# Forward stores moved to the sync queue and partly merged; phi's derivative rebuilt on GpSimd in the backward

## The chip, the cores and the metric

The kernel runs on one core of a Trainium2 chip. The core has a matrix engine (TensorE, PE), a vector engine (VectorE, DVE), a scalar engine for activations (ScalarE, ACT), a general engine (GpSimd, POOL) and a sync engine (SyncE, SP) that only issues DMAs. Every engine works through its own list of instructions in order; semaphores tie the lists together. DMAs are issued from SP and from ACT, each with a queue of its own, and are carried by 16 shared DMA engines. The metric is the device time of one execution in microseconds. A change of less than about 0.5% (12 us) can't be told from no change here.

## What is computed

Four attention blocks in a row on a sequence of 2048 tokens with 640 features (32 heads of 20), and then the gradients of all of it: of the input and of four weight matrices. Blocks 0 and 2 are linear attention (A), blocks 1 and 3 causal attention with a window of 256 (B). All data are bf16.

```python
def _A_ref(x, wqkv, wo):
    ...
    q, k, v = qkv[0], qkv[1], qkv[2]
    phi = lambda t: jnp.where(t > 0, t + 1, jnp.exp(t)) + 1e-6
    pq, pk = phi(q), phi(k)
    kv = jnp.einsum("bhsd,bhse->bhde", pk, v)
    z = jnp.einsum("bhsd->bhd", pk)
    num = jnp.einsum("bhqd,bhde->bhqe", pq, kv)
    den = jnp.einsum("bhqd,bhd->bhq", pq, z)[..., None] + 1e-6
    o = num / den
    return (lambda x, *d: x.transpose(*d))(o, 0, 2, 1, 3).reshape(B, S, D) @ wo
...
x = x + _A_ref(_layernorm(x, axis=-1), A_wqkv, A_wo)
x = x + _B_ref(_layernorm(x, axis=-1), B_wqkv, B_wo)
x = x + _A_ref(_layernorm(x, axis=-1), A_wqkv, A_wo)
x = x + _B_ref(_layernorm(x, axis=-1), B_wqkv, B_wo)
...
_out, _vjp = jax.vjp(_f, A_x, A_wqkv, A_wo, B_wqkv, B_wo)
_grads = _vjp(grad_out)
```

The derivative of phi is 1 where its argument is positive and exp of it elsewhere, that is min(exp(t), 1).

## The kernel before

The tokens are cut into 16 tiles of 128. Everything that the backward needs is written to DRAM by the forward and read back tile by tile.

**Forward** (`forward`), one program of about 806 us. `a_first` runs layer 0's layer norm and q, k, v over all tiles: the exponential of the projection goes to a tile `ee` (ACT, L457), is capped at 1 there (DVE, L458; the result is phi's derivative), and phi is put together from the two (L461) into `pp` for q and into the resident `pk` for k; v goes to the resident `vv`. `a_kv` sums the key-value products of all tiles into `mbd`. Then `ab_pass(0)` goes over the tiles once more and interleaves, for tiles some steps apart: layer 0's numerators (`a_num`), the output projection, layer 1's layer norm, q, k, v (`b_qkv`), its scores and values (`attn`: scores on PE into the PSUM ring `s_ps`, exponential on ACT at L617, masks on POOL and DVE, values on PE), its output projection, and `a_first` for layer 2. After a second `a_kv`, `ab_pass(2)` does the same without a following linear layer and stores the output x.

Nine kinds of store per tile are issued from ACT: pq, eq, pk, ek and v of a linear layer, its output o and the reciprocals `r32` of its denominators, and for a windowed layer o and the reciprocals `linv`. SP issues the stores of the layer norms `hn` and of `qkvp`, and all transposing DMAs (*flips*) that bring a tile into the layout that PE takes as weights: `hnTA`, `pqT`, `oTA`, `hnTB`, `QT`, `KT`, `oTB`, and `wT` for the transposed weights.

**Backward.** A short phase for layer 3's output projection (806 to 870 us), `B_attn_bwd(3)`, the phase `bwd_phase(3, 2, 1)`, `B_attn_bwd(1)`, and `bwd_phase(1, 0, None)`. Within such a phase, `lin_grads` of the linear layer reads tmp_dN, pk and v through flips (`dNT`, `pkT`, `vT`) and eq and ek by plain loads, multiplies the products by eq and ek on DVE (L1181) into `dqkv`; `tail` flips `dqkv` (`dqT`), multiplies it by the transposed weight `wq` (30 matmuls per tile, L839) into `dh`, and runs the layer norm's gradient: DVE L995, ACT L1002, POOL L1005 (`gw`), DVE L1007 (`gcar`). In layer 2's phase `local_dO` of layer 1 follows in the same loop, with POOL L1055 (`prod`); in layer 0's, the result is stored.

**What sets the order.** Each of the phases is written as a list of operations with reads and writes. A planner (`Sched.order`) gives every operation an assumed duration, simulates the five engines and one DMA channel, and emits the operations in the order in which they would start; each engine then keeps this order. For a DMA issue it assumes a time on the issuing engine: 1100 ns plus size for a flip, 330 ns for a copy on SP and 200 ns for one on ACT. An instruction that waits for its data holds up all that stands behind it on its engine.

Of the kernel before, what the change touches and what calls it, by code (L numbers as in the profile page):

```python
# [11 lines left out]
ALU = mybir.AluOpType  # L12
# [4 lines left out]
P = 128  # L17
# [15 lines left out]
def dve_ns(n):  # L33
    return 150 + 1.04 * n
# [26 lines left out]
class Sched:  # L61
# [39 lines left out]
    def order(self):  # L101
# [21 lines left out]
        while len(out) < len(self.ops):  # L123
# [50 lines left out]
class Kern:  # L174
    def __init__(self, ctx, tc, x0, A_wqkv, A_wo, B_wqkv, B_wo, grad_out, outs):
# [61 lines left out]
        self.ckv = self.const.tile([P, 3, 4 * DH], F32, name="ckv")  # L237
        nc.vector.memset(self.ckv[:, 0:2, :], self.c_att)
        nc.vector.memset(self.ckv[:, 2, :], 1.0)
# [69 lines left out]
    def forward(self):  # L309
# [4 lines left out]
        hch = CW // DH  # L314
        with ExitStack() as st:
# [5 lines left out]
            def ring(name, n, shape, dt=BF, **kw):  # L321
# [17 lines left out]
                wT=ring("wT", 1, [P, DT, P]), rt=ring("rt", 2, [P, H], F32), li=ring("li", 2, [P, H], F32),  # L339
            )  # L340
            pk = big.tile([P, TT, D], BF, name="pk")
            vv = big.tile([P, TT, D], BF, name="vv")
# [11 lines left out]
                   (("Wqkv_B", QT), ("Wqkv_A", QT), ("Wo_A", D), ("Wo_B", D))}  # L354
            S = Sched(tc, ahead=AHEAD)
# [79 lines left out]
            def a_qkv(l, tt, hnT):  # L435
# [3 lines left out]
                def chunk(ci):  # L439
                    def f():  # L440
# [4 lines left out]
                        if ci >= 4:  # L445
# [66 lines left out]
            def a_num(l, tt, oT):  # L512
                sv = self.sv[l]
                o = R["oA"].buf()
                rt = R["rt"].buf()

                def chunk(ci):
                    def f():
# [16 lines left out]
                        if ci == 0:  # L535
                            op("DVE", 190, lambda: nc.vector.tensor_scalar_add(rt.t, ps.t[:, CW:CW + H], 1e-6), [ps],
                               [rt])
                            op("DVE", 190, lambda: nc.vector.reciprocal(rt.t, rt.t), [], [rt])
                            dma("ACT", lambda: self.tm_view(sv["r32"])[:, tt, :], lambda: rt.t, 16 * KB, [rt], [])
# [3 lines left out]
                            in1=rt.t[:, ci * hch:(ci + 1) * hch].unsqueeze(2).to_broadcast([P, hch, DH]), op=ALU.mult),  # L543
                           [ps, rt], [(o, ci)])
# [53 lines left out]
            def attn(l, b, qT, kTs, vts, oT):  # L598
# [3 lines left out]
                pvs, lv, es = {}, R["li"].buf(), {}  # L602
# [918 lines left out]
```

## Time and profile before

| | us |
|---|---|
| median of 3 runs (lowest to highest) | 2367.98 (2361.93 to 2374.64) |
| span of the profiled execution | 2364.9 |
| PE, DVE, ACT, POOL busy | 2054.9, 1472.1, 1219.0, 850.2 |
| forward up to the last x store | about 806 |
| layer 3's projection phase | about 806 to 870 |
| attention backward, layers 3 and 1 | about 870 to 1190 and 1610 to 1960 |
| linear stage of layer 2 with layer 1's projection | about 1410 to 1540 |
| linear stage of layer 0 | about 2185 to 2305 |

A timeline row of the profile gives the start and the duration in microseconds, the engine, the line of the kernel, the operation, the tiles written and read, their shapes and how many instructions are merged; in brackets stands how long the engine had been idle and what ended that. ACTq and SPq are DMA issues of these engines; they are not counted as busy time. A DMA row of the list of issues gives the size of one and the median time from issue to landing. PE is busy 87% of the span, but each stage has its own limit, so the stages are read one by one.

### The profile page before, as it was taken

The numbers are of one execution on the slowest core, as the hardware profiler recorded it, in microseconds if no ns is written. First come the engines' busy times: TensorE is split into PE (matmuls) and PEld (weight loads), VectorE is DVE, ScalarE is ACT, GpSimd is POOL, SyncE is SP. The second block draws the span as 40 slices with busy tenths as digits, with TensorE's granted clock in tenths as the row PEclk, the third lists the DMA queues.
The fourth block names the chain that finished last, engine by engine and source line by source line (L and its number), as shares of the span: only waits on it lengthen the run. The fifth ranks groups of instructions, "written<-read, shape, count | busy, mean of one in ns | idle before, by whom it ended". The sixth has DMA issues, their size and how long they took to land. (4 is left out here: it accounts for less than half of the span.)

```text
span 2364.9 us, 68753 instructions
## 1 busy us (share of the span) xinstructions
PE 2054.9 (87%) x28146; PEld 1428.7 (60%) x28146; DVE 1472.1 (62%) x3120; ACT 1219.0 (52%) x1837; POOL 850.2 (36%) x1851
## 2 busy tenths in 40 slices
PE   5778888878888789898889979997989888997899
PEld 3555555555555457777756657754777775664664
DVE  5656676655565479989943328812998994443552
ACT  3527777716777328888822213312888882210330
POOL 1014454504555445555512203301555551220120
PEclk9989999989999789999999999997999998998999
DMA  7659999726666766777687779736666677878963
GB/s 245 196 134 194 202 212 204 178 93 151 138 151 139 188 178 131 125 130 130 136 173 177 163 189 208 166 94 151 130 126 134 124 139 154 192 178 193 189 153 102
DMA packets 937070, 377.91 MB, mean 160 GB/s; under 512 B 817072, under 2 KB 921136, under 8 KB 936496
## 3 DMA queue, kind: packets, MB, share of 16 engines
q1 hardware_dynamic: 856672, 299.45, 60.9%
q10 hardware_dynamic: 80080, 74.06, 9.7%
q8 instruction: 220, 3.60, 0.7%
q14 instruction: 98, 0.80, 0.1%
HBM read 115.34 MB, written 114.95 MB: 97 GB/s over the span
## 5 line engine op out<-in xcount | busy, mean ns | idle before, releaser
L1342 ACT ACTIVATE e_sb<-pair 128x768 bf16<-128x768 f32 x480 | 389.0, 812 | 123.7 <-PE pair L1322 116.0
L1357 DVE TENSOR_TENSOR ds_sb<-pair,e_sb 128x768 bf16<-128x768 f32 x480 | 436.4, 948 | 17.9 <-PE pair L1322 13.5
L617 ACT ACTIVATE e_sb<-s_ps 128x1536 bf16<-128x1536 f32 (+2 forms) x256 | 350.8, 1370 | 86.2 <-PE s_ps L612 42.9
L621 POOL TENSOR_SCALAR_AFFINE_SELECT e_sb<-e_sb 128x256 bf16<-128x256 bf16 x512 | 217.9, 448 | 491.1 <-ACT e_sb L617 467.0
L839 PE MATMUL mm_ps<-wq,dqT 128*128 128x320 bf16 x1920 | 284.9, 304 | 20.7 <-DMA dqT<-dqkv 20.7
L839 PEld LDWEIGHTS <-om 128*128 128x128 bf16 x1920 | 190.3, 100 | 166.5 <-DMA om<-o 9.9
L1349 POOL TENSOR_SCALAR_AFFINE_SELECT e_sb<-e_sb 128x256 bf16<-128x256 bf16 x448 | 182.1, 406 | 272.2 <-ACT e_sb L1342 263.6
L839 PE MATMUL mm_ps<-dqkv,om 128*128 128x480 bf16 x1280 | 270.8, 369 | 0.0
L1005 POOL TENSOR_TENSOR gw<-w,gcar 128x640 f32<-128x640 f32 x64 | 89.4, 1397 | 475.0 <-ACT w L1002 475.0
L839 PEld LDWEIGHTS <-dqT 128*128 128x128 bf16 x1920 | 186.6, 99 | 97.7 <-DMA dqT<-dqkv 22.9
L1346 POOL TENSOR_SCALAR_AFFINE_SELECT e_sb<-e_sb 128x256 bf16<-128x256 bf16 x512 | 206.5, 406 | 76.6 <-ACT e_sb L1342 75.2
L1386 PE MATMUL dqvk_ps<-Ksl,dsT 128*128 128x32 bf16 x2880 | 223.4, 177 | 3.0 <-DVE dqkv L1395 3.0
L987 ACT ACTIVATE dh<-mm_ps 128x320 f32<-128x320 f32 x128 | 55.9, 437 | 329.6 <-PE mm_ps L839 269.4
L1390 PE MATMUL dqvk_ps<-dOsl,e_sb 128*128 128x32 bf16 x2880 | 220.5, 176 | 0.9 <-issue 0.9
L1390 PE MATMUL dqvk_ps<-Qsl,ds_sb 128*128 128x32 bf16 x2880 | 220.3, 176 | 0.0
L1370 PE MATMUL dsT_ps<-ident,ds_sb 128*128 128x128 bf16 x2244 | 192.8, 223 | 29.0 <-ACT dsT L1374 25.2
L1322 PE MATMUL pair<-KTg,QTg 32*128 32x384 bf16 (+2 forms) x1024 | 164.1, 325 | 40.4 <-DVE ds_sb L1357 32.6
L1374 ACT COPY dsT<-dsT_ps 128x768 bf16<-128x768 bf16 x240 | 190.9, 795 | 11.9 <-PE dsT_ps L1370 5.8
L1370 PEld LDWEIGHTS <-ds_sb 128*128 128x128 bf16 x2244 | 140.2, 99 | 92.1 <-issue 88.6
L394 PE MATMUL mm_ps<-Wqkv_B,hnTB 128*128 128x320 bf16 x960 | 185.7, 312 | 3.8 <-ACT v_slab L584 2.9
L646 PEld LDWEIGHTS <-e_sb 128*128 128x128 bf16 x2880 | 131.1, 98 | 80.7 <-POOL e_sb L629 19.0
L1322 PE MATMUL pair<-VTg,dOTg 32*128 32x384 bf16 (+2 forms) x1024 | 164.2, 327 | 14.1 <-DMA dOTg<-dOpt 7.6
(153 smaller groups left out, 3721.5 us busy)
## 6 DMA issues: line engine op xcount, KB each, us to landing
qkvp<-qk_slab SPq DMA_DIRECT2D x32, 512.0 KB, 3.9
o<-o SPq DMA_DIRECT2D x64, 160.0 KB, 3.0
om<-o SPq DMA_DIRECT2D x20, 512.0 KB, 4.2
hn<-hn SPq DMA_DIRECT2D x64, 160.0 KB, 2.7
om<-hn SPq DMA_DIRECT2D x20, 512.0 KB, 4.8
qkvp<-v_slab SPq DMA_DIRECT2D x32, 256.0 KB, 3.1
dOpt<-slab ACTq DMA_DIRECT2D x32, 256.0 KB, 3.2
Ksl<-qkvp SPq DMA_DIRECT2D x16, 512.0 KB, 4.3
```

The costliest lines, as they stand in the source:

```text
L394: nc.tensor.matmul(ps.t[:, w0:w0 + width], lhsT=lhsT(), rhs=rhs(), start=start, stop=stop)
L617: op("ACT", av(4 * nkt * P), lambda: nc.scalar.activation(e.t[:, :, 0:nkt, :], s.t[:, :, 0:nkt * P].rearrange("p h (i q) -> p h i q", q=P) ...
L621: op("POOL", 440, lambda p_=p_: nc.gpsimd.affine_select(out=e.t[:, 2 * p_:2 * p_ + 2, nkt - 1, :], in_=e.t[:, 2 * p_:2 * p_ + 2, nkt - 1, ...
L839: nc.tensor.matmul(ps.t[:, w0:w0 + width], lhsT=lhsT(), rhs=rhs(), start=start, stop=stop)
L1322: nc.tensor.matmul(ps[:, i, c0:c0 + len(ks) * P], lhsT=ld[g][lhs][r, q * P:(q + 1) * P], rhs=ld[g][rhs][r, ks[0] * P:(ks[-1] + 1) * P], st ...
L1342: nc.scalar.activation(e, PR[h][:, :, 0:3 * P].rearrange("p i (j q) -> p i j q", q=P), ACT.Exp, scale=self.c_att)
L1346: nc.gpsimd.affine_select(out=e[:, :, j, :], in_=e[:, :, j, :], compare_op=ALU.is_ge, fill=0.0, base=0, pattern=[[0, 2], [-1, P]], channel ...
L1357: nc.vector.tensor_mul(DS[n][:, hs], PR.pop(h)[:, :, 0:3 * P].rearrange("p i (j q) -> p i j q", q=P), E[n][:, hs])
L1370: nc.tensor.transpose(ps[:, i, j, :], DS[n][:, 2 * p + i, j, :], self.ident)
L1374: (nc.vector.tensor_copy if h % 2 else nc.scalar.copy)(TSB[h], TPS.pop(h))
L1386: nc.tensor.matmul(a[:, 0, hh, :], lhsT=TSB[2 * n + hh // 2][:, hh % 2, j, :], rhs=ld[g]["K"][:, k, cs], start=(i == 0), stop=(i == len(dq ...
L1390: nc.tensor.matmul(a[:, 1 + x, hh, :], lhsT=src[n][:, hh, j, :], rhs=ld[g][rhs][:, q, cs], start=(i == 0), stop=(i == len(dkv) - 1))
```

## The change

In the forward, the stores of pq, both o, `r32`, `linv` and x are issued from SP, not from ACT. `r32` and `linv` are gathered over two tiles (RG = 2) and stored together. pk and v become the halves of one resident tile `kv`, and are stored with one DMA of 2560 bytes per row. eq and ek are no longer stored. In the backward, one flip of `kv` takes the place of the flips of pk and v. phi's derivative is made from the features: pq and the first half of kv are loaded into `ee`, and GpSimd computes min(phi - 1e-6, 1) in place. The planner's assumed issue times become 430 ns on SP and 385 ns on ACT. The constant `ckv`, used in the attention backward, is allocated after the forward.

```diff
-                    free[e] = t + (330 if e == "SP" else 200)
+                    free[e] = t + (430 if e == "SP" else 385)
...
-                pq=d.tile([T, D], BF, name=f"pq{l}"), pk=d.tile([T, D], BF, name=f"pk{l}"),
-                eq=d.tile([T, D], BF, name=f"eq{l}"), ek=d.tile([T, D], BF, name=f"ek{l}"),
-                v=d.tile([T, D], BF, name=f"v{l}"), o=d.tile([T, D], BF, name=f"o{l}"),
+                pq=d.tile([T, D], BF, name=f"pq{l}"),
+                kv=d.tile([T, 2 * D], BF, name=f"kv{l}"), o=d.tile([T, D], BF, name=f"o{l}"),
...
-            pk = big.tile([P, TT, D], BF, name="pk")
-            vv = big.tile([P, TT, D], BF, name="vv")
+            kv = big.tile([P, TT, 2 * D], BF, name="kv")
+            pk, vv = kv[:, :, 0:D], kv[:, :, D:2 * D]
...
-                                dma("ACT", lambda: self.tm_view(sv["v"])[:, tt, :], lambda: vv[:, tt, :], 160 * KB,
-                                    [("vv", tt, 4), ("vv", tt, 5)], [])
+                                dma("SP", lambda: self.tm_view(sv["kv"])[:, tt, :], lambda: kv[:, tt, :], 320 * KB,
+                                    [("pk", tt, 2), ("pk", tt, 3), ("vv", tt, 4), ("vv", tt, 5)], [])
...
-                            dma("ACT", lambda: self.tm_view(sv["pq"])[:, tt, :], lambda: p_.t[:, 0:D], 160 * KB,
+                            dma("SP", lambda: self.tm_view(sv["pq"])[:, tt, :], lambda: p_.t[:, 0:D], 160 * KB,
                                 [(p_, 0), (p_, 1)], [])
-                            dma("ACT", lambda: self.tm_view(sv["eq"])[:, tt, :], lambda: e.t[:, 0:D], 160 * KB,
-                                [(e, 0), (e, 1)], [])
-                        if ci == 3:
-                            dma("ACT", lambda: self.tm_view(sv["pk"])[:, tt, :], lambda: pk[:, tt, :], 160 * KB,
-                                [("pk", tt, 2), ("pk", tt, 3)], [])
-                            dma("ACT", lambda: self.tm_view(sv["ek"])[:, tt, :], lambda: e.t[:, D:2 * D], 160 * KB,
-                                [(e, 2), (e, 3)], [])
...
-                            dma("ACT", lambda: self.tm_view(sv["r32"])[:, tt, :], lambda: rt.t, 16 * KB, [rt], [])
+                            if i_ == RG - 1:
+                                dma("SP", lambda: self.tm_view(sv["r32"])[:, tt - i_:tt + 1, :], lambda: rt.t,
+                                    16 * RG * KB, [(rt, i) for i in range(RG)], [])
...
-                            dma("ACT", lambda: self.tm_view(sv["o"])[:, tt, :], lambda: o.t, 160 * KB,
+                            dma("SP", lambda: self.tm_view(sv["o"])[:, tt, :], lambda: o.t, 160 * KB,
...
-                            dma("ACT", lambda: self.tm_view(self.sv[l]["o"])[:, b, :], lambda: o.t, 160 * KB, ks, [])
-                            dma("ACT", lambda: self.tm_view(self.sv[l]["linv"])[:, b, :], lambda: lv.t, 16 * KB,
-                                [(lv, i) for i in range(H // 16)], [])
+                            dma("SP", lambda: self.tm_view(self.sv[l]["o"])[:, b, :], lambda: o.t, 160 * KB, ks, [])
+                            if i_ == RG - 1:
+                                dma("SP", lambda: self.tm_view(self.sv[l]["linv"])[:, b - i_:b + 1, :], lambda: lv.t,
+                                    16 * RG * KB, [(lv, i, j) for i in range(RG) for j in range(H // 16)], [])
...
-                                dma("ACT", lambda: xout[:, tt, :], lambda: x[:, tt, :], 160 * KB, [("x", tt)], [])
+                                dma("SP", lambda: xout[:, tt, :], lambda: x[:, tt, :], 160 * KB, [("x", tt)], [])
...
-                    for nm, src, size in (("dNT", self.tmp_dN, 192 * KB), ("pkT", sv["pk"], 160 * KB),
-                                          ("vT", sv["v"], 160 * KB)):
+                    for nm, src, size in (("dNT", self.tmp_dN, 192 * KB), ("kvT", sv["kv"], 320 * KB)):
...
-                    c["eq"], c["ek"] = load("eq", sv["eq"], tt), load("ek", sv["ek"], tt)
+                    c["ee"] = R["ee"].buf()
+                    for i, src in enumerate((sv["pq"], sv["kv"][:, 0:D])):
+                        dma("SP", lambda i=i: c["ee"].t[:, i, :], lambda src=src: self.tm_view(src)[:, tt, :], 160 * KB,
+                            [], [(c["ee"], i)])
+                        op("POOL", 900, lambda i=i: nc.gpsimd.tensor_scalar(
+                            out=c["ee"].t[:, i, :], in0=c["ee"].t[:, i, :], scalar1=1e-6, scalar2=1.0,
+                            op0=ALU.subtract, op1=ALU.min), [], [(c["ee"], i)])
...
-                            op("DVE", dve_ns(CW), lambda: nc.vector.tensor_mul(dst(), ps.t[:, 0:CW], e.t[:, e0:e0 + CW]),
-                               [ps, e], [("dqkv", tt, kind)])
+                            e, i = c["ee"], int(kind == "k")
+                            op("DVE", dve_ns(CW), lambda: nc.vector.tensor_mul(dst(), ps.t[:, 0:CW], e.t[:, i, e0:e0 + CW]),
+                               [ps, (e, i)], [("dqkv", tt, kind)])
```

More of the change, by code (lines that the diff above doesn't have):

```diff
@@ L236, in __init__ @@
             nc.vector.memset(t, 1.0)
-        self.ckv = self.const.tile([P, 3, 4 * DH], F32, name="ckv")
-        nc.vector.memset(self.ckv[:, 0:2, :], self.c_att)
-        nc.vector.memset(self.ckv[:, 2, :], 1.0)
         self.eps_t = self.const.tile([P, 1], F32, name="eps_t")
@@ L314, in forward @@
         hch = CW // DH
+        RG = 2
+        assert TT % RG == 0
         with ExitStack() as st:
@@ L338, in forward @@
                 st=ring("st", 2, [P, 2, nc.vector.BN_STATS_DIM], F32), mv=ring("mv", 2, [P, nc.vector.BN_AGGR_DIM], F32),
-                wT=ring("wT", 1, [P, DT, P]), rt=ring("rt", 2, [P, H], F32), li=ring("li", 2, [P, H], F32),
+                wT=ring("wT", 1, [P, DT, P]), rt=ring("rt", 2, [P, RG, H], F32), li=ring("li", 2, [P, RG, H], F32),
             )
-            pk = big.tile([P, TT, D], BF, name="pk")
-            vv = big.tile([P, TT, D], BF, name="vv")
+            kv = big.tile([P, TT, 2 * D], BF, name="kv")
+            pk, vv = kv[:, :, 0:D], kv[:, :, D:2 * D]
             x = big.tile([P, TT, D], BF, name="x")
@@ L514, in a_num @@
                 o = R["oA"].buf()
-                rt = R["rt"].buf()
+                i_ = tt % RG
+                if not i_:
+                    rts[0] = R["rt"].buf()
+                rt = rts[0]
                 def chunk(ci):
@@ L535, in f @@
                         if ci == 0:
-                            op("DVE", 190, lambda: nc.vector.tensor_scalar_add(rt.t, ps.t[:, CW:CW + H], 1e-6), [ps],
-                               [rt])
-                            op("DVE", 190, lambda: nc.vector.reciprocal(rt.t, rt.t), [], [rt])
-                            dma("ACT", lambda: self.tm_view(sv["r32"])[:, tt, :], lambda: rt.t, 16 * KB, [rt], [])
+                            op("DVE", 190, lambda: nc.vector.tensor_scalar_add(rt.t[:, i_, :], ps.t[:, CW:CW + H], 1e-6),
+                               [ps], [(rt, i_)])
+                            op("DVE", 190, lambda: nc.vector.reciprocal(rt.t[:, i_, :], rt.t[:, i_, :]), [], [(rt, i_)])
+                            if i_ == RG - 1:
+                                dma("SP", lambda: self.tm_view(sv["r32"])[:, tt - i_:tt + 1, :], lambda: rt.t,
+                                    16 * RG * KB, [(rt, i) for i in range(RG)], [])
                         op("DVE", vp(CW), lambda: nc.vector.tensor_tensor(
@@ L601, in attn @@
                 o = R["oB"].buf()
-                pvs, lv, es = {}, R["li"].buf(), {}
+                pvs, es, i_ = {}, {}, b % RG
+                if not i_:
+                    lis[0] = R["li"].buf()
+                lv = lis[0]
                 def scores(g):
@@ L651, in f @@
                             h0 = 16 * q
-                            li = lambda: lv.t[:, h0:h0 + 16]
-                            op("DVE", 200, lambda: nc.vector.reciprocal(li(), pv.t[:, :, DH]), [pv], [(lv, q)])
+                            li = lambda: lv.t[:, i_, h0:h0 + 16]
+                            op("DVE", 200, lambda: nc.vector.reciprocal(li(), pv.t[:, :, DH]), [pv], [(lv, i_, q)])
                             op("DVE", vp(16 * DH), lambda: nc.vector.tensor_tensor(
@@ L893, in bwd_phase @@
                         ("scr", 1, [P, D], BF), ("pq", 2, [P, D], BF), ("dNT", 2, [P, DT + 1, P], BF),
-                        ("pkT", 2, [P, DT, P], BF), ("vT", 2, [P, DT, P], BF), ("eq", 2, [P, D], BF), ("ek", 2, [P, D], BF)):
+                        ("kvT", 2, [P, 2 * DT, P], BF), ("ee", 2, [P, 2, D], BF)):
                     R[name] = ring(name, n, shape, dt)
@@ L1160, in f @@
                         ks = [k for k in range(DT) if not (self.band[k][1] <= e0 or self.band[k][0] >= e0 + CW)]
-                        src, rhs, key, col = {"q": ("dNT", mbdT, "mbdT", 0), "k": ("vT", dmbdT, "dmbdT", D),
-                                              "v": ("pkT", dmbd, "dmbd", 2 * D)}[kind]
+                        src, k0, rhs, key, col = {"q": ("dNT", 0, mbdT, "mbdT", 0), "k": ("kvT", DT, dmbdT, "dmbdT", D),
+                                                  "v": ("kvT", 0, dmbd, "dmbd", 2 * D)}[kind]
                         b = c[src]
@@ L1454, in run @@
         self.wq = self.persist2.tile([P, self.QTT, self.D], BF, name="wq")
+        self.ckv = self.persist2.tile([P, 3, 4 * DH], F32, name="ckv")
+        nc.vector.memset(self.ckv[:, 0:2, :], self.c_att)
+        nc.vector.memset(self.ckv[:, 2, :], 1.0)
         for l in (3, 1):
```

12 lines of the change are left out of this document (6 added, 6 removed).

## The prediction

> **What bounds the kernel now.** I read, in order, the busy time of each engine by stage, the chain of waits, and the timelines of ACT and SP, the queue that issues most DMAs. The rows of the first view give start:end, length, then busy us (count) of PE, weight loads, DVE, ACT, POOL, then granted clock, DMA share, GB/s.
>
> ```profile
> 22.00:128.00 106.00, 80.43 (x623) 54.20 (x622) 63.88 (x185) 54.60 (x133) 0.00 (x0) 0.97 0.67 202
> ...
> 190.00:470.00 280.00, 243.13 (x3871) 159.88 (x3868) 189.22 (x534) 206.63 (x273) 138.55 (x337) 0.98 0.94 200
> ...
> 1410.00:1540.00 130.00, 127.60 (x1135) 94.47 (x1136) 109.07 (x235) 40.69 (x109) 39.24 (x29) 0.99 0.85 185
> 2185.00:2305.00 120.00, 107.48 (x935) 78.13 (x936) 63.07 (x153) 40.54 (x108) 22.36 (x16) 0.97 0.82 172
> ```
>
> These are the stages that the change touches: layer 0's first linear pass; the interleaved pass over layers 1 and 2; and the two backward stages of the linear layers, layer 2 (PE full, DVE at 84%) and layer 0. The second interleaved pass (530 to 770 us) is a fifth; the two long attention stages of the backward are not touched. In the interleaved pass ACT shows 206.6 of 280 us, but DMA issues are not counted as busy. ACT's timeline there:
>
> ```profile
> 302.74 1.45 ACT L617 ACTIVATE e_sb<-s_ps 128x1536 bf16<-128x1536 f32 x1
> 303.75 0.33 ACTq L362 DMA_DIRECT2D r<-rt  x1
> 306.01 0.34 ACTq L362 DMA_DIRECT2D v<-vv  x1
> 306.40 0.42 ACT L584 CAST v_slab<-mm_ps 128x320 bf16<-128x320 f32 x1 [2.21 <-PE mm_ps L394]
> ...
> 306.72 1.46 ACT L617 ACTIVATE e_sb<-s_ps 128x1536 bf16<-128x1536 f32 x1
> ```
>
> Between 304.2 and 306.0 ACT stands before the store of v, which waits for its data; then comes a cast that PE waits for. Summed over the 280 us, issue rows cover 24 us in which no activation runs, and gaps directly ahead of an issue row another 27 (13 ahead of v, 11 ahead of ek). ACT is taken up for some 257 of 280 us. PE's waits that end on ACT come to 30 us (23.5 of them for score banks that the exponential L617 has not yet read).
>
> **The stores, in the forward.** 304 ACT stores go (nine kinds of 32, and 16 of x); SP gets 176: pq, kv, o twice, 32 each, x 16, and r32 and linv at 16 each for two tiles. The stores of eq and ek, 64 of 160 KB, vanish.
>
> First pass, 22 to 128 us: PE waits that end on ACT are 5.5 (pqT) + 3.7 (hnTA) + 3.1 + 0.6 + 0.3 = 13 us; ACT spends 22 us of the 106 on issue rows outside activations. SP is issuing for 45 of the first 150 us, so two more stores of about 0.4 us per tile hide there. Bounds 0 and -22; I take -10, most of the 13.
>
> Interleaved pass: the ACT side offers at most the 30 us of PE waits. SP decides how much is taken. Its rows cover 209.8 of the 280 us, 14.9 per tile (113 exponentials, 8 per tile, so 14.1 tiles of 19.8 us), and it waits 5.0 per tile. Five stores per tile come on top (pq, kv, two o, and half each of r32 and linv); the hn and qkvp stores there take 0.51 to 0.62 us on SP, so 2.8 more: 17.7 us of issue in a tile of 19.8. SP also has the flips (transposing DMAs) that feed PE, and these slow down behind stores:
>
> ```profile
> 307.14 0.45 SPq L362 DMA_DIRECT2D qkvp<-qk_slab  x1
> 307.68 1.98 SPq L366 DMA_TRANSPOSE oTA<-oA  x1
> ```
>
> An undisturbed flip issues in 1.2 us. So SP takes ACT's place near the bound: no waits at all would give 17.7 us per tile, -30 us; today's 5.0 would give 22.7, +41. In the backward's layer 2 stage SP's rows take 80 of 98 us, with 1.2 us of gaps per 8.2 us tile, so a crowded SP can run at short waits. I take 1.5 us: 19.2 per tile, -8 us. The DMA engines are no new bound: by packet records a 1280-byte packet takes 65 ns, so the 4,096 packets of eq and ek in this pass take 17 us off 16 engines, and the rest only changes queue.
>
> Second interleaved pass: two o, r32, linv and x leave ACT; issue rows outside activations are 14 us of 240. But the pace is the exchange of scores and exponentials through one PSUM ring (PE waits on L617 for 26.6 us), and most issues fall inside it. Bounds 0 and -14; I take -4. SP issues for 121 of 240 us and hides 3 us more per tile.
>
> The planner's new issue costs (430 and 385 ns) also reorder the work. The instruction lists of the two kernels show the same matmuls, and the same flips in each pass but one; I cost this at nothing, inside the bounds of the passes. The two ckv memsets move to the seam; by the slab memset's row (0.53 us for 512 words) they take 0.25 us of DVE, which waits for linv there anyway.
>
> **The seam at 806 us.** This is the change's cost. The last x store now stands on SP ahead of the backward's first loads: grad_out (320, then 640 and 1600 KB), Wo^T (800 KB), linv. Before, these were issued long before the forward ended, except linv:
>
> ```profile
> 786.51 0.93 SPq L829 DMA_DIRECT2D gcar<-in_grad_out_dram  x2
> ```
> ```profile
> 806.26 0.34 ACTq L362 DMA_DIRECT2D out_dram<-x  x1
> ```
> ```profile
> 806.28 0.44 PE L860 MATMUL mm_ps<-ident,gcar 128*128 128x128 bf16 x5 [0.58 <-DVE x L559]
> ```
> ```profile
> 813.68 1.28 DVE L1048 TENSOR_TENSOR slab<-mm_ps,linv 128x320 bf16<-128x320 f32 x3
> ```
>
> Now the first grad_out load can be issued at 806.6 and lands 2.8 us later (its own row), 3.2 us after PE wanted it. linv comes behind all of them, and a transfer waits for those ahead of it on its queue:
>
> ```profile
> x<-in_A_x_dram SPq DMA_DIRECT2D x1, 1920.0 KB, 14.1
> ...
> hn<-hnA SPq DMA_DIRECT2D x1, 160.0 KB, 6.0
> ```
>
> That x load was issued at about 1.9 us and landed at 16; the hn store, issued at 10.2, landed at 16.2. In the Trainium skill, "DMA: Bandwidth & Descriptors", section "Queues, rings and completion order", each DMA engine consumes a queue's descriptors in ring order; by that, too, linv comes last, and the trace agrees with the 6.0 us. 3.36 MB at the 250 GB/s of the two grad_out loads (2.24 MB in 9.0 us) is 13.4 us: linv lands near 821 instead of 806, and L1048 starts at 821 instead of 813.7, 7.3 us late. Six PSUM tiles hold PE's projections meanwhile. Bounds +3 (only the first load counts) and +11 (dWo's operand, queued behind linv, sets it); I take +7.
>
> **The backward.** Per tile two flips (pkT, vT) become one of ten blocks. Flips of 5, 8 and 15 blocks issue in 1.20, 1.25 and 1.51 us, so ten take about 1.35 in place of 2.6: SP wins 1.2 us per tile. The loads of pq and of k's half of kv take the place of eq and ek at the same size. In layer 0's stage, the chain of waits runs through SP and the flip of dqkv:
>
> ```profile
> 2232.93 1.20 SPq L833
> 2234.22 4.57 DMA dqT<-dqkv
> 2238.84 3.78 PE mm_ps L839 x15
> ```
>
> Fifteen tiles take 108.7 us by the gw rows, 7.24 each; where nothing is late (2247.9 to 2260.2) a tile takes 6.13. So at most 16.7 us can be won, and at least SP's own 5.5 us on the chain; I take -10. In layer 2's stage PE is busy 127.6 of 130 us: at most -2.
>
> New on POOL are 64 subtract-and-min operations of 128x640 bf16, two per tile. No row shows one. From below: selects of 140 and 256 elements take 343 and 406 ns, 0.54 ns per element, so 0.6 us at 640. From above: the two-input 128x640 operation, 1.40. I take 1.0, the 256-element select scaled up, as one input is nearer to it. The loads run two tiles ahead and POOL is busy 39 of 130 and 22 of 120 us, so the time itself hides. What may not hide is the port:
>
> ```profile
> 1435.21 1.34 POOL L1055 TENSOR_TENSOR prod<-slab,o 128x640 f32<-128x640 bf16 x1
> 1435.28 1.95 DVE L1007 SCALAR_TENSOR_TENSOR gcar<-hn,sm,gw 128x640 bf16<-128x640 bf16 x1 [0.35 <-POOL gw L1005]
> ```
>
> The same L1007 takes 0.89 us at 2232.4, with no POOL work beside it; here it ends 0.7 us after POOL does. DVE has 21 us free in the 130, so I take 0 for this stage, with bounds -2 and +11 (below).
>
> **Sum.** -10 - 8 - 4 + 7 - 10 + 0 = -25. The profiled span is 2364.9 us, the median of runs 2368.0, 3.1 above it, inside their spread. 2364.9 - 25 + 3.1 = 2343 us.
>
> **Rivals.** (1) *SP becomes the bound of the interleaved pass.* Stores that wait for data hold back the flips behind them, and today's 5.0 us of waits per tile stay: 22.7 us per tile, +41 in place of -8, so 2392 us. The whole turns slower once more than 3.3 us of waits per tile remain (21.0 us per tile, +17). For: SP's gaps today are waits for data. Against: the planner spaces the stores by 430 ns each and chooses its order by them. (2) *ACT was all of it*: the pass reaches 17.7 us per tile and the first pass wins 20: 2311 us. Against: it leaves SP no wait. (3) *The stores were hidden anyway*: the forward gains nothing, the last stage 5, the seam costs 7: 2370 us. For: PE is at 87% in the pass. (4) *The port lock*: each new POOL operation blocks a DVE operation for its 1.0 us. 2.0 us x 16 tiles = 32, less DVE's 21 free, +11 in layer 2's stage: 2354 us. Here a rule speaks against the change: the Trainium skill, "SBUF — State Buffer", section "Who interferes with whom", has a DVE operation with two SBUF inputs and a GpSimd operation that reads SBUF shut each other out for the whole instruction; the L1007 row agrees. (5) That eq and ek are not really saved can't be: their stores are absent from the changed kernel's instruction lists.
>
> **Chances.** Forecast 0.45, its own range 2325 to 2356; rival 1 0.17, rival 2 0.13, rival 3 0.13, rival 4 0.12. This kernel can tell about 0.5%, 12 us, from no change. Rival 4 lies at that edge and is halved: faster 0.45 + 0.13 + 0.06 = 0.64, same 0.13 + 0.06 = 0.19, slower 0.17. The range is 2308 to 2384: it takes in rivals 2, 3 and 4 and leaves out most of rival 1.
>
> **What would show it.** ACT's issue rows absent before 800 us, and PE's waits on L617 in the interleaved pass well under 23.5 us. SP's rows near 17.7 us per tile there, with gaps of 1 to 2: with 4 or more, or PE waits on hnTB, QT, KT or oTA, rival 1 holds. grad_out issued after the last x store, and L1048 first near 15 us after it. gw rows of the last stage 6.5 us apart. The new POOL operation near 1.0 us; L995 and L1007 stretched mean rival 4. The forecast is wrong if the pass over layers 1 and 2 grows, or if the seam costs over 11 us.

## The result, and the profile after

The changed kernel takes 2388.51 us (median of 4 runs, 2385.99 to 2390.78) against 2371.31 for the kernel before beside it (4 runs). The ratio is 1.0083, with a 95% interval of 1.0054 to 1.0111: slower, where faster was forecast. The profiled executions span 2384.2 and 2364.9 us. One execution of a later run, that of the planner's two prices, took 2451.61 us at a granted clock of 0.826 in place of 0.96; it is left out of that run's ratio, and its stages are not used. Every instruction from the feature pass on has moved by a few lines: `gw` is now L1006, `gcar` L1008, `prod` L1056, `slab` L1049, the product by the factor L1187; the new GpSimd operation is L1158.

To see where the 19.3 us went, each span was cut at rows that both traces have: the first masked sum after the key-value products of layers 0 and 2, the last addition to x, the first `slab` and the first score of the backward, the first and last row of the linear stages (the first `dmbd` to the last `gw`). Lengths in us, worked out from the starts of these rows:

| stage | before | after | change | forecast |
|---|---|---|---|---|
| first pass, layer 0 | 128.3 | 116.9 | -11.4 | -10 |
| first interleaved pass | 363.6 | 353.7 | -9.9 | -8 |
| second interleaved pass | 313.8 | 297.7 | -16.1 | -4 |
| seam, to the first `slab` | 8.0 | 13.6 | +5.6 | +7 (whole seam) |
| seam, to the first score | 52.3 | 59.1 | +6.8 | (above) |
| linear stage of layer 2 | 156.1 | 189.1 | +33.0 | 0 |
| linear stage of layer 0 | 145.5 | 158.8 | +13.3 | -10 |
| all the rest | 1197.3 | 1195.3 | -2.0 | 0 |

The forward does more than was asked of it; the two linear stages lose it all. The busy time by stage of the kernel after, in the stretches shown of the kernel before and with the same columns:

```profile
22.00:128.00 106.00, 89.34 (x786) 62.03 (x784) 68.20 (x201) 52.93 (x132) 0.00 (x0) 0.95 0.56 169
190.00:470.00 280.00, 249.34 (x3793) 162.29 (x3789) 192.83 (x540) 203.18 (x274) 131.75 (x321) 0.96 0.84 182
1410.00:1540.00 130.00, 110.53 (x910) 79.94 (x911) 86.08 (x200) 34.40 (x89) 94.09 (x48) 0.92 0.67 151
2185.00:2305.00 120.00, 98.19 (x854) 70.79 (x851) 57.64 (x139) 36.54 (x97) 87.45 (x41) 0.94 0.84 172
```

In the third row PE falls from 127.6 to 110.5 busy us of 130, and POOL (the last pair) rises from 39 to 94; in the fourth POOL goes from 22 to 87. POOL is not full at 94 of 130, yet something of it sets the pace. The group of the new operation on the page (busy us, mean ns of one, idle time before it) gives its price:

```profile
L1158 POOL TENSOR_SCALAR ee<-ee 128x640 bf16<-128x640 bf16 x64 | 161.5, 2524 | 124.3 <-DMA ee<-pq 110.2
```

2.52 us on average, where 1.0 was taken and 1.40 was the upper bound. POOL's timeline through two tiles of layer 2's stage:

```profile
1456.48 3.04 POOL L1158 TENSOR_SCALAR ee<-ee 128x640 bf16<-128x640 bf16 x1
1459.60 1.34 POOL L1056 TENSOR_TENSOR prod<-slab,o 128x640 f32<-128x640 bf16 x1
1461.31 2.35 POOL L1158 TENSOR_SCALAR ee<-ee 128x640 bf16<-128x640 bf16 x1 [0.37 <-DMA ee<-pq]
1465.15 1.40 POOL L1006 TENSOR_TENSOR gw<-w,gcar 128x640 f32<-128x640 f32 x1 [1.50 <-ACT w L1003]
1466.63 3.04 POOL L1158 TENSOR_SCALAR ee<-ee 128x640 bf16<-128x640 bf16 x1
1469.75 1.35 POOL L1056 TENSOR_TENSOR prod<-slab,o 128x640 f32<-128x640 bf16 x1
```

From one `prod` to the next are 10.15 us, against 8.17 to 8.19 before, where `gw` waits 5.48 us for ACT:

```profile
1443.38 1.35 POOL L1055 TENSOR_TENSOR prod<-slab,o 128x640 f32<-128x640 bf16 x1
1450.21 1.40 POOL L1005 TENSOR_TENSOR gw<-w,gcar 128x640 f32<-128x640 f32 x1 [5.48 <-ACT w L1002]
1451.57 1.35 POOL L1055 TENSOR_TENSOR prod<-slab,o 128x640 f32<-128x640 bf16 x1
```

After the change one `ee` operation of a tile stands between `gw` and `prod`, the other between `prod` and the next `gw`, where `gw` still waits 1.50 us for ACT. What ACT waits for is on DVE and ACT:

```profile
1456.43 0.88 DVE L1008 SCALAR_TENSOR_TENSOR gcar<-hn,sm,gw 128x640 bf16<-128x640 bf16 x1 [0.36 <-POOL gw L1006]
...
1460.98 0.82 DVE L1059 TENSOR_REDUCE dd<-prod 128x32 f32<-128x640 f32 x1 [3.03 <-POOL prod L1056]
...
1463.08 0.82 DVE L996 CUSTOM_DVE_ANT_0 scr<-dh,hn 128x640 bf16<-128x640 f32 x1
...
1463.95 0.15 DVE L1002 TENSOR_TENSOR sm<-sm,nrs 128x1 f32<-128x1 f32 x1
```
```profile
1464.15 0.92 ACT L1003 ACTIVATE w<-dh,sm,rs 128x640 f32<-128x640 f32 x1 [4.13 <-DVE sm L1002]
```

This closes a loop: DVE stands 3.03 us before `dd`, which needs `prod`; `sm` is behind `dd` in DVE's list; `w` needs `sm`; `gw` needs `w`; the `ee` operation is behind `gw` and `prod` behind that. Of the 10.15 us, 3.04 are the `ee` operation, and 7.1 the rest. A loop of 7.1 us fits under the 8.17 us that a tile took before (with PE busy for 98% of the stage), with 1.07 to spare.

The extra 0.69 us of the 3.04 goes with the 0.88 us `gcar` (L1008) that DVE had begun at 1456.43, 0.05 us ahead. The port lock of the prediction explains that; the rows themselves show only that the two overlap. Of the 64 operations 13 took 3.04 us, and each of these began while a `gcar` was running.

The tile shown is a typical one, but not all are alike. The stage has 11 tiles with the operation between two `prod` rows. From the first of these rows to the twelfth are 116.4 us, 90.1 before: 26.3 of the 33.0 us. In 8 of the 11 the operation in the loop took 3.04 us, in 3 it took 2.35. With 7.06 us for the rest of a tile, as in those of the 3 that take 9.41, that makes 109.0 us. Of the other 7.4, 6.0 lie in four tiles in which the operation ahead of `gw` waited for its load of pq (2.78 us at 1515.27) and `gw` could only begin behind it. A further 6.1 us lie ahead of the first `prod`.

At the seam, SP's timeline and PE's after the last x store:

```profile
768.86 0.34 SPq L361 DMA_DIRECT2D out_dram<-x  x1
769.25 0.43 SPq L830 DMA_DIRECT2D gcar<-in_grad_out_dram  x1
...
771.34 0.74 SPq L830 DMA_DIRECT2D linv<-linv  x1
772.12 9.01 SPq L830 DMA_DIRECT2D o<-o  x2
781.24 0.37 SPq L830 DMA_DIRECT2D om<-o  x1
```
```profile
772.48 0.71 PE L861 MATMUL mm_ps<-ident,gcar 128*128 128x128 bf16 x5 [4.18 <-DMA gcar<-in_grad_out_dram]
774.60 1.49 PE L840 MATMUL mm_ps<-WoB,gT 128*128 128x320 bf16 x5 [1.40 <-DMA WoB<-WoTB]
...
785.45 3.85 PE L840 MATMUL mm_ps<-gcar,om 128*128 128x320 bf16 x16 [6.30 <-DMA om<-o]
```

The loads are issued behind the x store as forecast, and PE waits 4.18 us for the first. But SP is then held 9.01 us in the two issues of `o`, so `om`, the operand of the weight gradient, is issued at 781.2 and PE waits 6.30 us more.

### The profile page after: what moved, and what is told of

Its sections match the earlier page's. It is cut to its first block, busy times and chain, and to the rows that moved or that the text cites. A ratio compares the mean times of both kernels' runs of the same rounds, so it can differ in the third digit from the quotient of the medians.

```text
span 2384.2 us, 68354 instructions
## 1 busy us (share of the span) xinstructions
PE 2065.0 (87%) x28146; PEld 1428.8 (60%) x28146; DVE 1464.8 (61%) x3120; ACT 1217.7 (51%) x1837; POOL 1012.5 (42%) x1915
## 5 line engine op out<-in xcount | busy, mean ns | idle before, releaser
L840 PE MATMUL mm_ps<-wq,dqT 128*128 128x320 bf16 x1920 | 290.1, 306 | 12.7 <-DMA dqT<-dqkv 10.8
L1158 POOL TENSOR_SCALAR ee<-ee 128x640 bf16<-128x640 bf16 x64 | 161.5, 2524 | 124.3 <-DMA ee<-pq 110.2
L1006 POOL TENSOR_TENSOR gw<-w,gcar 128x640 f32<-128x640 f32 x64 | 89.4, 1397 | 239.5 <-ACT w L1003 233.7
```

The costliest lines, as they stand in the source:

```text
L840: nc.tensor.matmul(ps.t[:, w0:w0 + width], lhsT=lhsT(), rhs=rhs(), start=start, stop=stop)
L1158: op("POOL", 900, lambda i=i: nc.gpsimd.tensor_scalar(out=c["ee"].t[:, i, :], in0=c["ee"].t[:, i, :], scalar1=1e-6, scalar2=1.0, op0=ALU.s ...
```

## The experiments

The theory T1: the length of the GpSimd operation paces the linear stages. Rivals: T2, its place in the list does (any operation there, behind a wait for a load, planned at 0.9 us); T3, it blocks VectorE at the port; T4, the loads and transposing loads of the stage are slow whoever works on them; T5, the stage is slow through what the forward left behind. The second set of runs asks what gained in the forward: fewer stores, the change of queue, or the planner's prices; and what the seam costs.

**The operation left out, fused, and shortened.** Without it, the factor is phi itself:

```diff
-                        op("POOL", 900, lambda i=i: nc.gpsimd.tensor_scalar(
-                            out=c["ee"].t[:, i, :], in0=c["ee"].t[:, i, :], scalar1=1e-6, scalar2=1.0,
-                            op0=ALU.subtract, op1=ALU.min), [], [(c["ee"], i)])
```

> The GpSimd operation on ee is taken out and nothing put in its place: the gradient is multiplied by phi itself, so the cut of the factor to 1 is left out of the computation. Theory T1 (the operation's own length, 2.35 us twice a tile in GpSimd's list ahead of gw and prod, paces the linear stages): the layer-2 linear stage falls from 189 us to about 156 as before, the layer-0 one from 159 to 145 or less, and the time from 2388 to about 2340 us. Rival T4 (what is slow is the factor's loads and the transposing loads beside it, whoever works on them): both stages stay within 5 us of 189 and 159 and the time stays above 2375 us. Rival T5 (the stage is long because of what the forward left, clock or DMA traffic): the same as T4.

Measured: 2334.67 us, ratio to before 0.9851 (0.9815 to 0.9887); layer 2's stage 159.4, layer 0's 138.3 us. T4 and T5 fall: the stage's loads and the forward are those of the changed kernel. (A late load counts only together with the operation that waits for it.)

Fused into the multiply on DVE (the operation above left out, and):

```diff
-  nc.vector.tensor_mul(dst(), ps.t[:, 0:CW], e.t[:, i, e0:e0 + CW])
+  nc.vector.scalar_tensor_tensor(out=dst(), in0=e.t[:, i, e0:e0 + CW], scalar=1.0, in1=ps.t[:, 0:CW],
+                                 op0=ALU.min, op1=ALU.mult)
```

> The factor is made inside the VectorE multiply that uses it (min of phi and 1, times the gradient, in one operation; the subtraction of 1e-6 is left out), no operation on GpSimd. T1: as the run without the operation, about 2340 us, plus what the two-step multiply costs more than the plain one: 4 chunks a tile, so 64 in all in a stage pair of 16 tiles; if each is longer by 0.2 us and on the path, 13 us. Rival T3 (VectorE is what the GpSimd operation blocks, and VectorE is the pace): giving VectorE more work helps less than leaving the work out, and the time stays above 2365 us. T4: above 2375 us.

Measured: 2333.30 us, ratio 0.9844 (0.9806 to 0.9882); stages 159.6 and 135.7 us. The two-step multiply has the same duration as the plain one, and its group in the trace (ns min/median/max) says so:

```profile
L1184 DVE SCALAR_TENSOR_TENSOR dqkv<-ee,mm_ps x128: 473/480/489, 1379.3 to 2252.0; 128x320 bf16<-128x320 bf16 x128
```

The plain multiply has a median of 481 ns. The minimum costs nothing there (the subtraction of 1e-6 is left out), and T3 in the form that DVE is the pace falls.

The operation on half of the columns (`[:, i, :]` becomes `[:, i, 0:D // 2]`):

> The same GpSimd operation at the same places of the list, but on the first 320 of 640 columns: for the other half the gradient's factor is phi without its cut. T1: the operation takes 1.2 to 1.4 us in place of 2.35, GpSimd's chain of a tile falls from 7.5-8.2 us to 5.3-6.0, under the 8.2 us a tile of the stage before, and the layer-2 stage falls to 160 us or less, the time to 2340-2355. Rival T2 (it is the place, not the length: gw and prod stand behind an operation that waits for a load): the stage stays at 180 us or more and the time above 2375 us.

Measured: 2354.36 us, ratio 0.9938 (0.9917 to 0.9959); stages 170.0 and 145.1 us. The time is where T1 put it, but layer 2's stage is 10 us longer than its 160; T2 isn't told apart by this alone. On 32 columns (`0:32`):

> The GpSimd operation at its place, on 32 of 640 columns: phi's cut is left out for the other 608. From 1.28 us at 320 columns and 2.35 at 640 it should take about 0.3 us. The layer-2 stage was 159.4 us without it, 170.0 at 1.28 us, 170.1 at 1.80 and 189.1 at 2.35. If its length alone counts, the stage is 159-162 us and the time 2334-2340. If any operation at that place costs some 10 us (T2: gw and prod behind one that waits for a load, and the planner's 0.9 us), the stage stays at 167-171 us and the time at 2345-2352.

Measured: 2337.27 us, ratio 0.9848 (0.9828 to 0.9869); stages 159.6 and 137.1 us. The place alone costs nothing: T2 falls. One step in place of two:

```diff
-  scalar1=1e-6, scalar2=1.0, op0=ALU.subtract, op1=ALU.min
+  scalar1=1.0, scalar2=None, op0=ALU.min
```

> The GpSimd operation keeps its 640 columns and its place but does one step (min with 1) in place of two (subtract 1e-6, then min); the subtraction is left out. Halving the columns halved its 2.35 us to 1.28. If GpSimd pays by element and step, one step takes 1.2 to 1.5 us and the time is that of the half-column run, 2350-2358 us; if it pays by element alone, it stays at 2.3 us or more and the time at 2380-2390.

Measured: 2360.45 us, ratio 0.9969 (0.9952 to 0.9985); stages 170.1 and 149.7 us; the operation takes 1.80 us, between the two prices that were written down. The operation's rows of the three (ns min/median/max), first 32 columns, then 320, then one step:

```profile
L1158 POOL TENSOR_SCALAR ee<-ee x64: 317/318/1015, 1191.8 to 2257.4; 128x32 bf16<-128x32 bf16 x64
```
```profile
L1158 POOL TENSOR_SCALAR ee<-ee x64: 1277/1278/1975, 1189.1 to 2270.4; 128x320 bf16<-128x320 bf16 x64
```
```profile
L1158 POOL TENSOR_SCALAR ee<-ee x64: 1797/1804/2428, 1188.5 to 2276.8; 128x640 bf16<-128x640 bf16 x64
```

From 32 to 640 columns the two-step form takes 3.34 ns per element ((2.346 - 0.318) / 608) above a fixed 0.21 us, and 320 columns lie on that line. The second step costs 0.54 us of it. The longest of each is 0.6 to 0.7 us over the median; these, too, began beside a DVE operation with two inputs. Now the loop can be tested on single tiles. POOL's timeline of the half-column run:

```profile
1443.06 1.97 POOL L1158 TENSOR_SCALAR ee<-ee 128x320 bf16<-128x320 bf16 x1
1445.11 1.35 POOL L1056 TENSOR_TENSOR prod<-slab,o 128x640 f32<-128x640 bf16 x1
...
1452.10 1.28 POOL L1158 TENSOR_SCALAR ee<-ee 128x320 bf16<-128x320 bf16 x1
1453.46 1.34 POOL L1056 TENSOR_TENSOR prod<-slab,o 128x640 f32<-128x640 bf16 x1
```

The tile whose inner operation took 1.28 us is 8.35 us long (1445.11 to 1453.46); the next, with 1.97 at the port, 9.26 (to 1462.72); a tile of the one-step run, with 1.80, 8.64 (1446.68 to 1455.32); in the changed kernel, with 3.04, 10.15. Taking the operation away leaves 7.07, 7.29, 6.84 and 7.11 us: the loop is some 7.1 us plus one operation, and a tile gets longer than the 8.17 us before once the operation, with its wait at the port, takes more than 1.07. On 32 columns it takes 1.01 at the port, and the tile 8.09 (1444.21 to 1452.30). This is also why 1.28 and 1.80 us gave the same stage. Of the 11 inner operations of the stage, 10 of the shorter ones began behind `gcar` and took 1.97 us; all 11 of the longer ones took 1.80, because they began ahead of it, and there `gcar` paid:

```profile
1453.55 1.80 POOL L1158 TENSOR_SCALAR ee<-ee 128x640 bf16<-128x640 bf16 x1
```
```profile
1453.62 1.33 DVE L1008 SCALAR_TENSOR_TENSOR gcar<-hn,sm,gw 128x640 bf16<-128x640 bf16 x1 [0.35 <-POOL gw L1006]
```

From the first `prod` to the twelfth are 101.5 us on 320 columns, 100.0 with one step and 90.9 on 32 columns.

**The planner told the true price** (`op("POOL", 900` becomes `2400`):

> Only the planner's price of the GpSimd operation is changed, from 900 to 2400 ns; the work is the same. T1 (the sum of GpSimd's list, 7.5 us a tile, plus its own place ahead of gw): the order may take up to the 2 us of GpSimd's waits per tile of the layer-2 stage, so the stage ends between 165 and 189 us, and the time between 2365 and 2390 us; it does not come to the 2334 us of the kernel without the operation. T2 (only the place in the list is wrong, because the planner took 0.9 us): with the true price the stage falls to 160 us and the time to 2340 us or less.

Measured: 2372.83 us, ratio 1.0008 (0.9990 to 1.0026). Layer 0's stage falls from 158.8 to 143.3 us: there the order was part of it. Layer 2's is 185.0, and the stage before it (from its first `gw`) is 7.0 us longer: nothing is won there. In layer 2's stage all 11 operations in the loop now take 3.04 us, and in these tiles `gw` is no longer held up by a late load; from the first `prod` to the twelfth are 112.4 us. The order accounts for 15 of the 46 us that the two stages lost; the rest stays with the length.

**The seam.** The fused kernel, with the late stores back on ACT (o, linv and x of the last two tiles):

```diff
+  late = "ACT" if l == 3 and b >= TT - 2 else "SP"
-  dma("SP", lambda: self.tm_view(self.sv[l]["o"])[:, b, :], ...
+  dma(late, lambda: self.tm_view(self.sv[l]["o"])[:, b, :], ...
...
-  dma("SP", lambda: xout[:, tt, :], ...
+  dma("ACT" if tt >= TT - 2 else "SP", lambda: xout[:, tt, :], ...
```

> The fused multiply, and the last two tiles' stores of o, linv and x in the last forward layer issued by ScalarE again, so that gcar, the weights and linv of the first backward layer are issued on SP without them in front. If the seam's +12.4 us (13.6 against 8.0 up to the first slab, 59.1 against 52.3 behind it) come from SP issuing those loads behind the late stores, 5 to 10 us of it come back: about 2330-2335 us, 5 to 10 us under the fused kernel alone. If it comes from the bytes in flight or from the order behind the first slab, nothing comes back, and ScalarE's end of the forward gets 1 to 3 us longer.

Measured: 2320.96 us, ratio 0.9795 (0.9758 to 0.9832), 12.3 under the fused kernel. The seam is 8.2 and 52.7 us, against 8.0 and 52.3 before: all of it came back. The forward's end moved from 770.0 to 773.4, which is within what kernels with the same forward show (below). The gain is over the 5 to 10 us expected. SP's timeline there shows the loads ahead of the end:

```profile
770.53 0.37 SPq L832 DMA_DIRECT2D linv<-linv  x1
770.94 2.17 SPq L832 DMA_DIRECT2D o<-o  x1
```

ACT stores the last x at 773.93, after these.

**What gained in the forward.** The changed kernel, all forward stores on ACT, merged and without eq and ek:

```diff
-  dma("SP", lambda: self.tm_view(sv["kv"])[:, tt, :], lambda: kv[:, tt, :], 320 * KB,
+  dma("ACT", lambda: self.tm_view(sv["kv"])[:, tt, :], lambda: kv[:, tt, :], 320 * KB,
...
```

> As the changed kernel, but all forward stores are issued by ScalarE again, merged as they are and without eq and ek. If the forward's gain (805.7 to 768.3 us) comes from the change of queue, most of it is lost: the forward ends at 790 us or later. If it comes from there being fewer stores (160 of 304 left) and from the planner's order, it ends within 8 us of 768. The seam in either case goes back to about 8 and 53 us, since the last stores no longer stand on SP ahead of the first backward loads; the linear stages stay at 189 and 159 us. Time: 2375-2380 us if fewer stores are the gain, 2395 or more if the queue is.

Measured: 2363.67 us, ratio 0.9987 (0.9969 to 1.0006), 25 us under the changed kernel (2375 to 2380 was expected). Of the 304 stores 176 are left, not 160. The forward ends at 761.7, earlier than with SP: first pass 115.5 (with SP 116.9), first interleaved pass 341.4 (353.7), second 304.8 (297.7). So in the long pass the queue change cost 12 us, in the last it brought 7. How far single lengths can be trusted is shown by the changed kernel and the six runs that alter the backward alone: their forwards have the same order of instructions, and they end between 768.3 and 775.2, with 352.4 to 358.5 us for the first interleaved pass and 297.5 to 301.7 for the second. So the cost is 11 to 17 us, the gain 3 to 7. The list of waits (us in total, times, longest) between 180 and 445 us, first of the changed kernel, then of this one:

```profile
PE mm_ps L393 <- DMA hnTB<-hnB: 8.2, 7, 2.1
PE mm_ps L393 <- DMA oTA<-oA: 3.7, 3, 1.6
PE mm_ps L393 <- DMA hnTA<-hnA: 1.6, 1, 1.6
```
```profile
PE mm_ps L393 <- DMA hnTB<-hnB: 1.0, 1, 1.0
PE mm_ps L393 <- DMA oTA<-oA: 0.7, 2, 0.4
```

PE's 13.5 us of waits for flips become 1.7. This is the mechanism of rival 1, stores in front of the flips on SP, at some 12 us where the rival needed 49 (from -8 to +41).

The kernel before, with the two planner prices alone (SP 330 to 430 ns, ACT 200 to 385):

> The kernel before with the planner's two issue prices alone changed (SP 330 to 430 ns, the others 200 to 385). If the order that these make is part of the forward's gain, the forward ends earlier than 805.7 us: by 5 us or more in the first pass and the two interleaved passes together, above all in the second interleaved pass, which gained 16.1 where 4 was forecast. If they do nothing, every stage stays within 2 us and the time within 0.3% of 2371. With all stores still on ScalarE at a higher price, a third outcome is a slower forward.

Measured: 2352.66 us, ratio 0.9935 (0.9909 to 0.9960). The stages are read from a second run:

> The kernel before with the two planner prices again, for a profile of its stages. Its time is 2353 against 2369 us. If the prices alone made the second interleaved pass shorter (the gain there was 16.1 where 4 was forecast), that pass takes 300 us or less here and the other stages stay within 3 us; if they shorten the first passes, the first pass is under 125 us or the interleaved one under 358.

Measured: 2354.84 us, ratio 0.9911 (0.9888 to 0.9935). First pass 135.2 (before 128.3), first interleaved pass 355.8 (363.6), second 300.3 (313.8): the prices alone bring 13.5 of the 16.1 us of the second pass, and 7.8 in the first interleaved one. The expectation said nothing of a longer first pass beside them. In the second pass, PE's waits for the exponential, before (520 to 780 us) and with the prices (520 to 770):

```profile
PE s_ps L612 <- ACT e_sb L617: 27.8, 66, 1.6
```
```profile
PE s_ps L612 <- ACT e_sb L617: 21.5, 61, 0.9
```

About as many waits, with a longest of 0.9 in place of 1.6 us, which suggests that the score blocks come more evenly; it makes 6.3 of the 13.5 us.

With this run the way from the kernel before to the changed one has three steps: the prices (this run), fewer and merged stores (the run with all stores on ACT, at the same prices), and the queue. The forward's end goes from 805.7 to 791.3, 761.7 and 768.3 us. The same wait of PE, in the first interleaved pass, was 23.5 us before; with the prices (190 to 470 us), with fewer stores on ACT besides, and in the changed kernel (both 180 to 445) it is:

```profile
PE s_ps L612 <- ACT e_sb L617: 18.2, 37, 1.9
```
```profile
PE s_ps L612 <- ACT e_sb L617: 4.8, 12, 0.6
```
```profile
PE s_ps L612 <- ACT e_sb L617: 3.2, 9, 0.5
```

So it is the step with fewer stores that rids PE of its waits for ACT; whether by the stores of eq and ek that vanish or by the merging was not separated. The reverse, the changed kernel with the old prices:

> The changed kernel with the planner's issue prices of the kernel before (330 and 200 ns). If the order that the prices make carries the forward's gain, the forward ends at 780 us or later and the time is 2395 us or more; if the removed and merged stores carry it, the forward ends within 5 us of 768 and the time is within 0.3% of 2388.

Measured: 2395.13 us, ratio 1.0086 (1.0065 to 1.0107). The new prices gave 1.0083. The forward ends at 775.3, 7 later, at the edge of the 768.3 to 775.2 that the same forward shows: with the merged stores on SP, no gain from the prices can be told. So the second pass is short with merged stores on SP under the old prices (299.2) and with all the old stores on ACT under the new ones (300.3): either brings most of the 16 us, and they don't add. Of the two outcomes written down, the first (780 or later) is not reached, and the second (within 5 us of 768) is missed by 2, which is less than that spread. Why these orders are better beyond the evener scores stays open.

**Put together.** The fused kernel with late stores on ACT, and the stores of the first pass and of the first interleaved pass on ACT too (layer 0's and 1's o, r32 and linv, kv and pq):

```diff
-  dma("SP", lambda: self.tm_view(sv["o"])[:, tt, :], lambda: o.t, ...
+  dma("ACT" if l == 0 else "SP", lambda: self.tm_view(sv["o"])[:, tt, :], lambda: o.t, ...
...
-  late = "ACT" if l == 3 and b >= TT - 2 else "SP"
+  late = "ACT" if l == 1 or b >= TT - 2 else "SP"
```

> The fused kernel with the late stores on ScalarE, and besides the stores of the first pass and of the interleaved pass over layers 1 and 2 (kv, pq, and layer 0's and 1's o, r32, linv) issued by ScalarE; only the second interleaved pass stores from SP. If SP's share of the stores cost the first interleaved pass its flips (353.7 us with SP, 341.4 with ScalarE), that pass falls to 342-345 us, the second stays at 298-301, and the time is 2306-2312 us, the fastest of all. If the 12 us came from something else in that kernel, the time stays at 2321.

Measured: 2310.91 us (2308.68 to 2315.87), ratio 0.9735 (0.9718 to 0.9752): the fastest. The first interleaved pass takes 339.5 us, the second 301.8, the seam 9.0 and 52.3.

## Why the prediction was wrong

**The step that failed is the price of the GpSimd operation.** The prediction took 1.0 us, "the 256-element select scaled up, as one input is nearer to it", with 1.40 as the upper bound. It is 2.35, and 3.04 beside a DVE operation at the port. Neither row bounds it: a select steps at 0.54 ns per element, this two-step operation at 3.34, and the two-input operation of the same shape takes 1.34 to 1.40 us. Fewer inputs did not mean cheaper. In the Trainium skill, "GPSIMD Engine Reference", section "4.1 Engine selection", one-input work on GpSimd is called roughly line-rate; the 2.35 us beside 1.34 for two inputs don't bear that out here, and the measurement decides.

**"The time itself hides" was reckoned from POOL's busy share** (39 of 130 us). By the loop it would have hidden at 1.0 us, with 0.07 to spare, only where it didn't wait at the port; with 0.69 us of wait, as in 8 of the 11 tiles, it would not have, and neither at the 1.40 that the same text called possible. Over the 11 tiles, operations of 2.35 us make 13.4 of the 26.3 us, the port 5.5, and late loads 6.0. Idle time on an engine covers work only where the idle time is not itself a wait in the loop: of the two operations, the one that stands ahead of `gw` was nearly free where its load was in time, and the one behind it cost its whole length beyond 1.07 us.

**Layer 0's linear stage**, forecast -10, became +13.3 through the same operation; 15.5 us of it went with the order that the planner's 0.9 us made, and which wait that order set was not followed here. With the derivative fused the stage is 135.7, 9.8 under before, and without it 138.3, 7.2 under: the term was about right and was buried. The merged flip, to which the prediction put it, was not timed alone.

**Rival 4** had the right two parties, but in the changed kernel mostly the wrong sufferer: `gcar` keeps its 0.88 us where it begins first, and the GpSimd operation, which comes second, waits 0.69; in the one-step run it is the other way round. The Trainium skill, "SBUF — State Buffer", section "Who interferes with whom", has a DVE operation with two SBUF inputs and a GpSimd operation that reads SBUF contend for a shared port pair, and calls this an exclusive lock; the rows of 3.04 and 2.35 agree nearly (`gcar` had 0.83 us to go). The rows of the one-step run don't: `gcar` ends at 1454.95, 0.40 us ahead of the operation's end.

**The seam**, forecast +7 with bounds +3 and +11, is +12.4, and goes wholly with the late stores (the seam is back at +0.6 with them on ACT). The prediction's own sign of being wrong, a seam of over 11 us, is met. linv's lateness was sized about right: the first `slab` comes 5.6 us later after the forward's end, not 7. What the text named as its upper bound, the operand of dWo, came on top instead of in its place: SP held 9.01 us in the issues of `o` and PE 6.30 us for `om`.

**The forward** was forecast at -22 and came to -37.4. The first pass and the first interleaved pass came in at their terms (-11.4 and -9.9), and the tile of the latter at 19.3 us (106 intervals of its exponentials, 8 a tile, from 188.8 to 445.0) where 19.2 stood. SP's rows come to 17.3 us of such a tile and its gaps to 2.1, where 17.7 and 1.5 were taken. But the reason given was that ACT is rid of its stores, and that is not what the runs show. With fewer, merged stores left on ACT the pass is 12 us shorter still. ACT was relieved by the step with fewer stores; those that moved went in front of the flips. So the -9.9 is in part luck: the three steps are -7.8 (prices), -14.4 (fewer stores) and +12.3 (queue), and in the first pass +6.9, -19.7 and +1.4. The second pass, at -16.1 in place of -4, was missed at "I cost this at nothing": the planner's prices by themselves brought 13.5 us there.

Taken together: 33.0 + 23.3 (layer 0's +13.3 for -10) + 5.4 (seam) - 15.4 (forward) - 2.0 (the rest) = 44.3 us, the distance from the forecast's -25 to the span's +19.3.

## What to carry to other kernels

Work put on an engine with idle time is free only up to the slack of the loop it stands in: follow one tile round the engines in the timeline, add the new operation, and compare with the pace of the engine that is full. An operation whose exact form has no row in the trace has no price yet; before moving work to such an engine, look whether an instruction that is there already has a free second step. And a planner's cost constant is an edit of its own: time it alone.

## What the runs showed that was not expected

- A two-step operation with two constants on GpSimd takes 0.21 us + 3.34 ns per element (0.318, 1.278 and 2.346 us at 32, 320 and 640 columns); with one step 1.80 us at 640. The two-input product of 640 columns takes 1.34.
- Where `gcar` on DVE began 0.05 us ahead of the operation on GpSimd, the operation took 0.69 us more; where the one-step operation began 0.07 us ahead, `gcar` took 0.45 more.
- On VectorE, the minimum with a constant ahead of a multiply from PSUM is free: 480 against 481 ns for 128x320.
- Two prices in the planner, with the same 28146 matmuls and the same numbers of DVE, ACT and POOL instructions, made the kernel before 0.7 to 0.9% faster (0.9935 and 0.9911 in two sets of runs).
